# Attention and two expert layers on one core: the weighted sums in fp32, two heads in one pass of the array

## The chip, the cores and the metric

The kernel runs on one core of a Trainium2 chip. The metric is device time in microseconds (us), the median of several runs. The core has five engines with a queue each: TensorE (PE in the profile, with PEld for the loading of its stationary operand), VectorE (DVE), ScalarE (ACT), GpSimd (POOL) and SyncE (SP), which here only starts DMA transfers. SBUF is the working memory of 128 partitions; PSUM is the small memory into which PE writes. An engine works off its queue in order and waits on semaphores for the others.

## The reference

```python
def _attn_ref(q, k, v):                     # (4, 8, 576, 64) each
    q_rot, k_rot = (rotate(q), rotate(k))   # rotary embedding over the 64 columns
    scores = scale * np.matmul(q_rot, k_rot.transpose(0, 1, 3, 2))
    scores = scores - np.max(scores, axis=-1, keepdims=True)
    attn = np.exp(scores)
    attn = attn / (np.sum(attn, axis=-1, keepdims=True) + 1e-09)
    return np.matmul(attn, v).astype(np.float32)

def reference(...):
    x = attention output as (2304, 512)
    h = np.maximum(x @ w_in, 0.0); x = h * h @ w_out           # 512 -> 2048 -> 512
    e_idx = np.argmax(x @ w_gate + modality_bias[modality_id], axis=1)   # 8 experts
    out[mask] = gate_w[mask, None] * (np.maximum(x[mask] @ w1[e], 0.0) @ w2[e])
```

All is fp32, and the choice of the expert depends on small differences, so the kernel keeps close to fp32 throughout: it mostly splits an operand into a high part in the type fp32r and a low part (the rest), and adds up several products.

## The kernel before, in words

**Attention.** The 32 heads are worked in 16 pairs; the two heads of a pair lie in partitions 0 to 63 and 64 to 127. For each pair the program does, by the names in its table:

- `ldq`, `ldk`, `ldv` load; `aq` to `cq` and `ak` to `ck` are the rotary embedding (L213, L215, mostly on POOL); `qh`, `ql`, `kh`, `kl` split into high and low parts, and small transfers `qd`, `kd` move halves to other partitions.
- `sc0` to `sc8` are nine score tiles of 128 rows by 576 columns (L275). Tiles 0 to 3 are head 0, 4 to 7 head 1, tile 8 the 64 last rows of both. They go through two PSUM buffers in turn, in the order 3, 1, 2, 0, 4, 5, 6, 7, 8.
- `mx` takes the maximum of a tile (L280, DVE), `ex` its exponential and the sum of a row (L291, ACT), which frees the PSUM buffer.
- `tr` transposes the exponentials in groups of four 128x128 blocks (L333; L324 for the corner); `m00` to `m13` are eight main groups (first digit the head), `rk`, `rq` and `rr` the remainders. They go through four PSUM buffers called `b`, shared with the weighted sums.
- `eh` copies a group out of PSUM on ACT as the high part, `el` subtracts it on DVE for the low part (L197, L202); both lie in `et0`, `et1` and `rk`. `vhi` (ACT) and `vlo` (POOL) split the values.
- `pv00`, `pv01`, `pv10`, `pv11` are the weighted sums (L367), for head and half of the 576 columns: five chunks of 128 rows times the high and the low part of the exponentials, ten matmuls of 128x288. The stationary operand holds the high part of the values in 64 columns and the low part in 64 more, so the result has two halves that have yet to be added.
- `p1` copies the result out of PSUM (ACT). In pairs 0 to 3 (the first batch row, whose first 512 tokens are block 0 of the next layer) `p2` adds the halves on DVE, and `xn`, `xh`, `xl` normalize and split. In the other pairs `xr` stores both halves, and they are added (`xsum`) when the next layer reads them.
- `sa` (L299, POOL) and `srec` (DVE) prepare the reciprocals of the sums, `sev` and `rst` store them.

What sets the order is a table of times (`FIRST`, `SECOND`, `THIRD`, `PLAN` for pairs 0, 1, 2 and 3, and the rest): a step of pair p stands at its time plus 18 p, all steps are sorted by that number, and each goes into its engine's queue in that order ("T" PE, "V" DVE, "A" ACT, "P" POOL, "D" SP). The numbers are no promise: an engine starts a step when its operands and buffers are ready and the step before it is done.

**Expert layers.** `TAIL` mixes the first layer's weights (loaded as 64-bit floats, put together from two words) into the attention's last pairs. Then the first layer runs over five blocks of tokens, 16 steps each (L706, L740), and the second over the chosen experts (L1024, L1047).

Of the kernel before, what the change touches and what calls it, by code (L numbers as in the profile page):

```python
# [1289 lines left out]
```

## Time and profile before

| | us |
|---|---|
| median of 3 runs | 969.63 (967.72 to 970.1) |
| the profiled execution | 971.64 |
| its span, first to last instruction | 969.9 |
| PE busy | 903.1 (93%) |
| DVE busy | 679.6 (70%) |
| ACT busy | 530.4 (55%) |
| POOL busy | 370.9 (38%) |
| first and last maximum of a score tile | 23.1 and 310.4 |

The attention's steady part lasts from about 140 to 310 us, and the expert layers take the rest. PE's records overlap: matmuls are pipelined, a record lasts longer than the distance to the next, and a busy PE is not necessarily a full one. A wait shown in brackets is idle time of that engine right before the instruction, with the engine and operation that ended it.

### The profile page before, as it was taken

The page shows a single profiled execution, that of the slowest core. Times are in us where ns is not written, and L with a number is a line of the kernel's source. Part 1 is how long each engine was busy: PE and PEld are TensorE (multiplying, and loading weights), DVE is VectorE, ACT ScalarE, POOL GpSimd, SP SyncE. Part 2 cuts the span into 40 slices and gives each one's busy share as a digit, 9 for nine tenths or more (in the row PEclk, how much of TensorE's full clock was granted, in tenths as well). Part 3 has the DMA queues.
Part 4 walks back from the last instruction along what each step waited for, and adds up shares of the span by engine and source line. Part 5 has one row for each costly group of instructions (what it writes and reads, how often), then busy time and mean ns, then how long its engine had stood idle before and what let it go on. Part 6 is the DMA issues. An engine that isn't in the chain of part 4 may idle for free. (4 is left out here: it accounts for less than half of the span.)

```text
span 969.9 us, 15018 instructions
## 1 busy us (share of the span) xinstructions
PE 903.1 (93%) x5210; PEld 789.7 (81%) x5210; DVE 679.6 (70%) x1258; ACT 530.4 (55%) x1090; POOL 370.9 (38%) x287
## 2 busy tenths in 40 slices
PE   0888889999999989999999999999999999999996
PEld 0777888898888866787888888888988889999995
DVE  5789988998989899957647764664473956666650
ACT  3788878888989877532233223222343345555551
POOL 6787877787874466612003100100010124112011
PEclk9999999999999999999999999999999999999998
DMA  7556656746655556562005002100151267777630
GB/s 234 163 147 180 182 146 154 210 139 191 219 150 161 186 181 205 135 197 64 1 1 163 12 1 70 39 1 1 44 177 63 87 194 255 239 229 230 205 107 34
DMA packets 55714, 130.83 MB, mean 135 GB/s; under 512 B 11968, under 2 KB 16592, under 8 KB 55632
## 3 DMA queue, kind: packets, MB, share of 16 engines
q1 hardware_dynamic: 52592, 120.10, 41.3%
q0 software_dynamic: 3040, 9.70, 2.7%
q8 instruction: 43, 0.70, 0.3%
q14 instruction: 39, 0.32, 0.1%
HBM read 97.12 MB, written 19.21 MB: 120 GB/s over the span
## 5 line engine op out<-in xcount | busy, mean ns | idle before, releaser
L712 ACT ACTIVATE r<-h 128x512 f32<-128x512 f32 (+1 forms) x80 | 44.2, 552 | 216.6 <-PE h L706 199.8
L706 PE MATMUL h<-xs,w 128*128 128x512 f32 (+1 forms) x660 | 145.5, 369 | 6.8 <-DVE w L557 5.5
L706 PEld LDWEIGHTS h<-xs,w 128*128 128x128 f32 x660 | 115.1, 188 | 31.9 <-DVE w L557 9.3
L275 PE MATMUL sc<-kh,q 128*128 128x288 f32 (+2 forms) x336 | 98.8, 329 | 36.7 <-ACT kh L197 20.9
L720 DVE SCALAR_TENSOR_TENSOR h<-h,r 128x512 f32<-128x512 f32 (+1 forms) x80 | 51.5, 644 | 113.5 <-ACT r L712 113.2
L740 PE MATMUL y<-w,gh 128*128 128x512 f32 x396 | 122.6, 391 | 0.0
L291 ACT ACTIVATE e<-sc,nmx 128x576 f32<-128x576 f32 x144 | 107.0, 744 | 26.3 <-DVE nmx L280 25.9
L280 DVE TENSOR_REDUCE nmx<-sc 128x1 f32<-128x576 f32 x144 | 106.8, 751 | 17.5 <-PE sc L275 16.5
L978 DVE TENSOR_TENSOR w<-eraw,w 128x1024 fp32r<-128x1024 f32 x64 | 78.4, 1225 | 33.5 <-ACT w L977 33.4
L333 PE MATMUL b<-ident,e 128*128 128x128 f32 x640 | 91.8, 283 | 10.2 <-DVE et L202 4.2
L275 PEld LDWEIGHTS sc<-kh,q 128*128 128x128 f32 x336 | 62.9, 197 | 46.5 <-issue 23.3
L202 DVE TENSOR_TENSOR et<-b,et 128x512 fp32r<-128x512 f32 (+1 forms) x160 | 94.2, 626 | 8.2 <-ACT et L197 6.3
L275 PE MATMUL sc<-kl,q 128*128 128x288 f32 (+2 forms) x336 | 90.7, 304 | 0.0
L333 PEld LDWEIGHTS b<-ident,e 128*128 128x128 f32 x640 | 75.1, 145 | 18.8 <-PE b L324 5.7
L740 PEld LDWEIGHTS y<-w,gh 128*128 128x128 f32 x396 | 73.3, 188 | 14.4
L197 ACT ACTIVATE et<-b 128x512 fp32r<-128x512 f32 (+1 forms) x160 | 83.0, 561 | 2.9 <-PE b L333 2.5
L367 PE MATMUL b<-et,vs 128*128 128x288 f32 x512 | 78.4, 295 | 0.1
L740 PE MATMUL y<-w,gl 128*128 128x512 f32 x198 | 77.1, 389 | 0.0
L1024 PEld LDWEIGHTS h<-ye,w 128*128 128x128 f32 x576 | 74.0, 189 | 3.7
L1054 POOL DMA_INDIRECT out<-ob,six x19 | 21.6, 1138 | 139.8 <-ACT ob L1053 106.8
L752 DVE SCALAR_TENSOR_TENSOR junk<-ysb,wgb 128x512 f32<-128x512 f32 x96 | 75.0, 835 | 0.0
L1024 PE MATMUL h<-ye,w 128*128 128x256 f32 x576 | 74.8, 280 | 0.0
(219 smaller groups left out, 1851.6 us busy)
## 6 DMA issues: line engine op xcount, KB each, us to landing
eraw<-wexp SPq DMA_DIRECT2D x64, 512.0 KB
wraw<-wio SPq DMA_DIRECT2D x32, 512.0 KB
rawq<-qx SPq DMA_DIRECT2D x15, 576.0 KB
rawk<-kx SPq DMA_DIRECT2D x15, 576.0 KB
xT<-xo SPq DMA_DIRECT2D x24, 288.0 KB
kh<-kh SPq DMA_DIRECT2D x45, 144.0 KB
vraw<-v SPq DMA_DIRECT2D x16, 320.0 KB
q<-ql SPq DMA_DIRECT2D x32, 144.0 KB
```

The source lines that it names most:

```text
L197: nc.scalar.activation(out=out, in_=in_, func=ACTF.Copy)
L202: on[eng].tensor_tensor(out=out, in0=in0, in1=f32(hi), op=ALU.subtract)
L275: nc.tensor.matmul(out=o[:, x:x + w], lhsT=q[:, hd, q0:q0 + 128], rhs=k[:, hd, y:y + w], start=(n == 0), stop=(n == len(ops) - 1))
L280: nc.vector.tensor_reduce(out=m, in_=sc(p, j)[:, :, 0:HS], axis=AX.XY, op=ALU.max, negate=True)
L291: nc.scalar.activation(out=e(p)[:, o:o + S].rearrange("p (a b) -> p a b", a=2), in_=sc(p, j)[:, :, 0:HS], func=ACTF.Exp, bias=live[p, f"nm ...
L333: nc.tensor.transpose(t[:, i * 128:(i + 1) * 128], x[:, o:o + 128], ident)
L367: nc.tensor.matmul(out=o, lhsT=lhsT.rearrange("p a b -> p (a b)"), rhs=rhs, start=(c == 0 and i == 0), stop=(c == 4 and i == 1))
L706: nc.tensor.matmul(out=h, lhsT=w[:, a, k * 128:(k + 1) * 128], rhs=xs[b, k][:, c], start=(k == 0 and i == 0), stop=(k == 3 and i == 2))
L740: nc.tensor.matmul(out=yp[t], lhsT=g[a][:, t * 128:(t + 1) * 128], rhs=w[:, c, 512:1024], start=(f == 0 and i == 0), stop=(f == NFC - 1 an ...
L752: nc.vector.scalar_tensor_tensor(out=junk, in0=ysb[j], scalar=1.0, in1=wgb[e], op0=ALU.mult, op1=ALU.mult, accum_out=lg[:, j, e:e + 1])
L978: nc.vector.tensor_tensor(out=w[:, 1], in0=r, in1=f32(w[:, 0]), op=ALU.subtract)
L1024: nc.tensor.matmul(out=h, lhsT=w[:, a, k * 128:(k + 1) * 128], rhs=x[:, c], start=(k == 0 and i == 0), stop=(k == 3 and i == 2))
```

## The change

- The exponentials are copied out of PSUM once, in fp32 (`ev` in place of `eh` and `el`): of the eleven groups, `m02`, `m03`, `m10`, `m11`, `rq` and `rr` by ACT, `m00`, `m01`, `m12`, `m13` and `rk` by DVE (in pairs 4 and on). `et0`, `et1`, `rk`, the values and the result are double buffered.
- The values aren't split (`vhi` and `vlo` go).
- The weighted sums are two groups, `pv0` and `pv1`, one for each half of the columns. A group has ten fp32 matmuls with a stationary operand of 64 columns; head 0 writes partitions 0 to 63, head 1 partitions 64 to 127 of one PSUM tile, and the two heads alternate. The groups stand in the table where `pv10` and `pv11` stood.
- The result is whole: `u0` (DVE) and `u1` (ACT) copy it out, `p2`, the zero fills and `xsum` go, and the store and the later loads move half as much.

Of the table a few entries show what moves:

```diff
-    "trm02": (-69.906, "T"), "mx7": (-69.636, "V"), "ehm02": (-69.532, "A"), "elm02": (-69.257, "V"),
+    "evm02": (-69.532, "A"), "trm00": (-69.043, "T"), "trm03": (-68.699, "T"), "trm01": (-68.235, "T"),
...
-    "pv00": (-61.627, "T"), "elm10": (-61.115, "V"), "elm13": (-60.595, "V"), "pv01": (-60.561, "T"),
-    "rst": (-59.097, "D"), "p101": (-57.141, "A"), "pv10": (-56.563, "T"), "p100": (-56.461, "A"),
+    "rst": (-59.097, "D"), "pv0": (-56.563, "T"), "u0": (-55.931, "V"), "pv1": (-53.486, "T"), "u1": (-52.986, "A"),
```

The code:

```diff
-        rk_t = sb.tile([128, 2, SK], F32R, name="rk", bufs=1)
+        rk_t = [sb.tile([128, SK], F32, name=f"rk{i}", bufs=1) for i in range(2)]
...
-        def vraw(p):
-            return get(p, "vraw", [128, 10, D], F32, 1)
-
-        def vs(p):
-            return get(p, "vs", [128, 10, 2, D], F32R, NVS)
+        def vt(p):
+            return get(p, "v", [128, 10, D], F32, 2)
-            nc.sync.dma_start(out=vraw(p), in_=v[p])
-
-        def vhi(p, eng):
-            copy(eng, vs(p)[:, :, 0], vraw(p))
-
-        def vlo(p, eng):
-            sub(eng, vs(p)[:, :, 1], vraw(p), vs(p)[:, :, 0])
+            nc.sync.dma_start(out=vt(p), in_=v[p])
...
                 nc.tensor.transpose(t[:, i * 128:(i + 1) * 128], x[:, o:o + 128], ident)
 
         def et(p, hd):
-            return get(p, f"et{hd}", [128, 2, 4, S], F32R, 1)
-
-        def evac(p, g):
-            t = tb(p, g)
+            return get(p, f"et{hd}", [128, 4, S], F32, 2)
+
+        def evac(p, eng, g):
+            t, rk = tb(p, g), rk_t[p % 2]
             if g == "rk":
-                return [(t, rk_t[:, :, 64:S])]
-            if g == "rr":
-                return [(t[0:64, 0:64], rk_t[0:64, :, S:640]), (t[0:64, 64:128], rk_t[64:128, :, 0:64])]
-            if g == "rq":
+                parts = [(rk[:, 64:S], t)]
+            elif g == "rr":
+                parts = [(rk[0:64, S:640], t[0:64, 0:64]), (rk[64:128, 0:64], t[0:64, 64:128])]
+            elif g == "rq":
                 t = t.rearrange("p (c x) -> p c x", c=4)
-                return [(t[:, :, 0:64], et(p, 0)[:, :, :, 512:S]), (t[:, :, 64:128], et(p, 1)[:, :, :, 0:64])]
-            hd, c = int(g[1]), int(g[2])
-            return [(t, et(p, hd)[:, :, c, 64 * hd:64 * hd + 512])]
-
-        def ehi(p, eng, g):
-            for t, d in evac(p, g):
-                copy("A", d[:, 0], t)
-
-        def elo(p, eng, g):
-            for t, d in evac(p, g):
-                sub("V", d[:, 1], t, d[:, 0])
-
-        def pv(p, eng, hd, n):
-            o = get(p, f"u{hd}{n}", [128, HS], F32, 4, ps, "b")
-            r0 = 64 * (1 - hd) + n * HS
+                parts = [(et(p, 0)[:, :, 512:S], t[:, :, 0:64]), (et(p, 1)[:, :, 0:64], t[:, :, 64:128])]
+            else:
+                hd, c = int(g[1]), int(g[2])
+                parts = [(et(p, hd)[:, c, 64 * hd:64 * hd + 512], t)]
+            for o, i in parts:
+                copy(eng, o, i)
+
+        def pv(p, eng, n):
+            o = get(p, f"u{n}", [128, HS], F32, 4, ps, "b")
             for c in range(5):
-                for i in range(2):
+                for hd in range(2):
+                    r0 = 64 * (1 - hd) + n * HS
                     if c < 4:
-                        lhsT, rhs = vs(p)[:, 2 * c + hd], et(p, hd)[:, i, c, n * HS:n * HS + HS]
+                        lhsT, rhs = vt(p)[:, 2 * c + hd], et(p, hd)[:, c, n * HS:n * HS + HS]
                     else:
-                        lhsT, rhs = vs(p)[:, 8 + hd], rk_t[:, i, r0:r0 + HS]
-                    nc.tensor.matmul(out=o, lhsT=lhsT.rearrange("p a b -> p (a b)"), rhs=rhs,
-                                     start=(c == 0 and i == 0), stop=(c == 4 and i == 1))
+                        lhsT, rhs = vt(p)[:, 8 + hd], rk_t[p % 2][:, r0:r0 + HS]
+                    nc.tensor.matmul(out=o[64 * hd:64 * hd + 64], lhsT=lhsT, rhs=rhs, start=(c == 0), stop=(c == 4))
 
         def xo(p):
-            return get(p, "xo", [128, 2, S], F32, NXO)
-
-        def pv1(p, eng, hd, n):
-            u, c = live[p, f"u{hd}{n}"], slice(n * HS, n * HS + HS)
-            if p >= 4:
-                copy(eng, xo(p)[:, hd, c], u)
-            else:
-                a, b = 64 * (1 - hd), 64 * hd
-                copy(eng, xo(p)[b:b + 64, 1, c], u[a:a + 64])
-
-        def pv2(p, eng, hd, n):
-            b, c = slice(64 * hd, 64 * hd + 64), slice(n * HS, n * HS + HS)
-            x = xo(p)
-            nc.vector.tensor_tensor(out=x[b, 0, c], in0=live[p, f"u{hd}{n}"][b], in1=x[b, 1, c], op=ALU.add)
-            if n == 1:
-                nc.vector.memset(x[b, 1, N0:S], 0.0)
+            return get(p, "xo", [128, S], F32, 2)
+
+        def take(p, eng, n):
+            copy(eng, xo(p)[:, n * HS:n * HS + HS], live[p, f"u{n}"])
 
         def xr(p, eng):
             b, h = divmod(p, 4)
             if b == 0:
-                nc.sync.dma_start(out=xT[h, :, :, N0:S], in_=xo(p)[:, :, N0:S])
-                return
-            for i in range(2):
-                nc.sync.dma_start(out=xT[h, :, i, b * S:b * S + S].rearrange("(g d) t -> d g t", g=2),
-                                  in_=xo(p)[64 * i:64 * i + 64])
+                nc.sync.dma_start(out=xT[h, :, 0, N0:S], in_=xo(p)[:, N0:S])
+            else:
+                nc.sync.dma_start(out=xT[h, :, 0, b * S:b * S + S], in_=xo(p))
...
         def xraw(b, k):
             t0, n = BLOCKS[b]
             if b == 1:
-                t = wts.pool.tile([128, 2, n], F32, name="xraw", tag="wraw", bufs=NRAW)
-                nc.sync.dma_start(out=t, in_=xT[k, :, :, t0:t0 + n])
-                raws[b, k] = t[:, 0], t[:, 1]
+                t = wts.pool.tile([128, n], F32, name="xraw", tag="wraw", bufs=NRAW)
+                nc.sync.dma_start(out=t, in_=xT[k, :, 0, t0:t0 + n])
+                raws[b, k] = t
                 return
             x = t2([128, n], F32, "xraw")
             if k == 0:
-                rbs[b] = sb.tile([128, 2, n], F32, name="rbs", tag="xs", bufs=5)
-            r, y = rbs[b][:, 0], rbs[b][:, 1]
+                rbs[b] = sb.tile([128, n], F32, name="rbs", tag="xs", bufs=5)
             nc.sync.dma_start(out=x, in_=xT[k, :, 0, t0:t0 + n])
-            nc.sync.dma_start(out=y, in_=xT[k, :, 1, t0:t0 + n])
-            raws[b, k] = x, y
-            xrec(b, k, r)
+            raws[b, k] = x
+            xrec(b, k, rbs[b])
...
-        def xsum(b, k, eng):
-            x, y = raws[b, k]
-            eng.tensor_tensor(out=x, in0=x, in1=y, op=ALU.add)
```

On PE, this is pair 12 before, from the transposes of its last main group (the four of `ident`) on: score tile 0 of the next pair, the first group of weighted sums, tile 4, and the second group (the tile of exponentials `et_3219` is head 0's).

```order
L333 MATMUL b<-ident,e_89 128x128 x4
L275 MATMUL sc<-kh_86,q_84 128x288
L275 MATMUL sc<-kl_88,q_84 128x288
L275 MATMUL sc<-kh_86,q_84 128x288
L275 MATMUL sc<-kl_88,q_84 128x288
L367 MATMUL b<-et_3219,vs 128x288 x8
L367 MATMUL b<-rk,vs 128x288 x2
L275 MATMUL sc<-kh_86,q_84 128x288
L275 MATMUL sc<-kl_88,q_84 128x288
L275 MATMUL sc<-kh_86,q_84 128x288
L275 MATMUL sc<-kl_88,q_84 128x288
L367 MATMUL b<-et_3219,vs 128x288 x8
```

And the same place after, from the last matmul of tile 0 on: tile 4, tile 5, and the first rows of the group `pv0`, whose `et_2708` is head 0's and `et_2777` head 1's.

```order
L245 MATMUL sc<-kl_88,q_84 128x288
L245 MATMUL sc<-kh_86,q_84 128x288
L245 MATMUL sc<-kl_88,q_84 128x288
L245 MATMUL sc<-kh_86,q_84 128x288
L245 MATMUL sc<-kl_88,q_84 128x288
L245 MATMUL sc<-kh_86,q_84 128x288
L245 MATMUL sc<-kl_88,q_84 128x288
L245 MATMUL sc<-kh_86,q_84 128x288
L245 MATMUL sc<-kl_88,q_84 128x288
L332 MATMUL b<-et_2708,v 64x288
L332 MATMUL b<-et_2777,v 64x288
L332 MATMUL b<-et_2708,v 64x288
```

The first group stood between tile 0 and tile 4; now tiles 0, 4 and 5 follow each other, and the group stands behind tile 5, with both heads in turn.

On DVE, the same pair before: the maxima of tiles 5, 6 and 7 (the three in one row), then the subtractions of three groups, the maximum of tile 8, two more, and the maximum of tile 3 of the next pair.

```order
L280 TENSOR_REDUCE nmx<-sc 128x1 x3
L202 TENSOR_TENSOR et_3219<-b,et_3219 128x512 x3
L280 TENSOR_REDUCE nmx<-sc 128x1
L202 TENSOR_TENSOR et_3219<-b,et_3219 128x512
L202 TENSOR_TENSOR rk<-b,rk 128x512
L280 TENSOR_REDUCE nmx<-sc 128x1
L302 RECIPROCAL e_89<-e_89 128x9
L202 TENSOR_TENSOR et_3295<-b,et_3295 128x512
L280 TENSOR_REDUCE nmx<-sc 128x1
L202 TENSOR_TENSOR et_3295<-b,et_3295 128x512
L202 TENSOR_TENSOR et_3219<-b,et_3219 128x4x64
```

And after: the maxima of tiles 5 and 6, the copy of the result of the pair before (`xo`), tile 7, and the copies between the maxima.

```order
L250 TENSOR_REDUCE nmx<-sc 128x1 x2
L178 COPY xo<-b 128x288
L250 TENSOR_REDUCE nmx<-sc 128x1
L178 COPY et_2708<-b 128x512
L250 TENSOR_REDUCE nmx<-sc 128x1
L178 COPY et_2708<-b 128x512
L178 COPY rk_91<-b 128x512
L250 TENSOR_REDUCE nmx<-sc 128x1
L272 RECIPROCAL e_89<-e_89 128x9
L250 TENSOR_REDUCE nmx<-sc 128x1
L178 COPY et_2777<-b 128x512
```

Between the maximum of tile 8 and that of tile 3 there are still two operations (`m01`'s and `rk`'s evacuation), copies now; ahead of tile 8's maximum one remains of three.

## Rows read from the trace of the kernel before

**Rows 1.** windows: busy us of PE, PEld, DVE, ACT, POOL; clock; DMA; GB/s

```profile
139.70:310.40 170.70, 161.53 (x1221) 152.37 (x1222) 154.61 (x256) 153.29 (x383) 127.88 (x97) 1.00 0.60 170
...
440.00:970.00 530.00, 518.03 (x2762) 447.08 (x2762) 304.88 (x641) 195.10 (x328) 69.56 (x60) 0.99 0.31 100
```

**Rows 2.** timeline of POOL: start us, us, engine, line, operation, [idle before]

```profile
139.69 0.24 POOL L299 TENSOR_SCALAR e<-e 128x9 f32<-128x9 f32 x1 [1.93 <-ACT e L291]
...
260.91 0.24 POOL L299 TENSOR_SCALAR e<-e 128x9 f32<-128x9 f32 x1 [0.50 <-ACT e L291]
...
266.88 1.44 POOL L215 TENSOR_TENSOR rawq<-rawq 128x576 f32<-128x576 f32 x1
...
274.13 1.56 POOL L202 TENSOR_TENSOR vs<-vraw,vs 128x640 fp32r<-128x640 f32 x1 [2.03 <-PE b L333]
...
278.07 0.24 POOL L299 TENSOR_SCALAR e<-e 128x9 f32<-128x9 f32 x1 [1.00 <-ACT e L291]
...
312.10 0.24 POOL L299 TENSOR_SCALAR e<-e 128x9 f32<-128x9 f32 x1 [2.65 <-ACT e L291]
```

**Rows 3.** timeline of DVE, the cycle from 261 to 278 us

```profile
268.36 1.66 DVE L199 CAST q<-rawq 128x576 fp32r<-128x576 f32 x1 [0.18 <-POOL rawq L215]
...
276.32 0.75 DVE L280 TENSOR_REDUCE nmx<-sc 128x1 f32<-128x576 f32 x1
```

**Rows 4.** timeline of ACT, the same cycle

```profile
261.82 0.74 ACT L291 ACTIVATE e<-sc,nmx 128x576 f32<-128x576 f32 x1
...
265.27 0.74 ACT L291 ACTIVATE e<-sc,nmx 128x576 f32<-128x576 f32 x1
...
271.52 0.74 ACT L291 ACTIVATE e<-sc,nmx 128x576 f32<-128x576 f32 x1 [0.94 <-DVE nmx L280]
```

**Rows 5.** timeline of PE, the same cycle

```profile
255.25 0.40 PE L275 MATMUL sc<-kh,q 128*128 128x288 f32 x1 [0.44 <-ACT e L291]
...
264.87 1.22 PE L367 MATMUL b<-et,vs 128*128 128x288 f32 x8
...
266.18 0.36 PE L275 MATMUL sc<-kh,q 128*128 128x288 f32 x1
...
268.12 0.29 PE L275 MATMUL sc<-kh,q 128*128 128x288 f32 x1
...
268.65 1.22 PE L367 MATMUL b<-et,vs 128*128 128x288 f32 x8
...
269.97 0.29 PE L275 MATMUL sc<-kh,q 128*128 128x288 f32 x1
...
271.56 0.42 PE L367 MATMUL b<-rk,vs 128*128 128x288 f32 x2
272.40 0.40 PE L275 MATMUL sc<-kh,q 128*128 128x288 f32 x1 [0.42 <-ACT e L291]
...
273.03 1.91 PE L333 MATMUL b<-ident,e 128*128 128x128 f32 x16
274.70 0.51 PE L275 MATMUL sc<-kh,q 128*128 128x288 f32 x2
```

**Rows 6.** groups by line, whole span: busy us, mean ns, then idle before

```profile
L202 DVE TENSOR_TENSOR et<-b,et 128x512 fp32r<-128x512 f32 (+1 forms) x160 | 94.2, 626 | 8.2 <-ACT et L197 6.3 <-PE b L367 1.0
...
L197 ACT ACTIVATE et<-b 128x512 fp32r<-128x512 f32 (+1 forms) x160 | 83.0, 561 | 2.9 <-PE b L333 2.5
```

**Rows 7.** timeline of PE in the early cycles, tile 7 of two pairs

```profile
74.60 0.40 PE L275 MATMUL sc<-kh,q 128*128 128x288 f32 x1 [0.72 <-ACT e L291]
...
132.38 0.40 PE L275 MATMUL sc<-kh,q 128*128 128x288 f32 x1 [2.17 <-ACT e L291]
```

**Rows 8.** line L333, the transposes: what PE waited for, us, times

```profile
  DVE xo L384: 3.5, 7
```

**Rows 9.** by stretch, columns as in Rows 1

```profile
55.00:60.00 5.00, 2.95 (x17) 2.17 (x16) 4.14 (x8) 3.72 (x9) 3.67 (x5) 0.82 1.00 269
...
130.00:135.00 5.00, 2.83 (x17) 2.62 (x16) 3.39 (x5) 3.33 (x8) 2.87 (x3) 0.83 0.78 182
```

More of the change, by code (lines that the diff above doesn't have):

```diff
@@ L27 @@
 N0 = 512
-BLOCK0 = ("p200", "p201", "p210", "p211", "rld", "xn", "xh", "xl", "xst")
+BLOCK0 = ("rld", "xn", "xh", "xl", "xst")
 HS = S // 2
 SK = S + 64
-RAW, NVS, NXO = 1, 1, 1
+RAW = 1
 NT = NTOK // 128
@@ L390, in xr @@
             if b == 0:
-                nc.sync.dma_start(out=xT[h, :, :, N0:S], in_=xo(p)[:, :, N0:S])
-                return
-            for i in range(2):
-                nc.sync.dma_start(out=xT[h, :, i, b * S:b * S + S].rearrange("(g d) t -> d g t", g=2),
-                                  in_=xo(p)[64 * i:64 * i + 64])
+                nc.sync.dma_start(out=xT[h, :, 0, N0:S], in_=xo(p)[:, N0:S])
+            else:
+                nc.sync.dma_start(out=xT[h, :, 0, b * S:b * S + S], in_=xo(p))
         def xn(p, eng):
-            x = xo(p)[:, 0, 0:N0]
+            x = xo(p)[:, 0:N0]
             on[eng].tensor_tensor(out=x, in0=x, in1=rb(p), op=ALU.mult)
@@ L404, in xhi @@
         def xhi(p, eng):
-            copy(eng, xh(p)[:, 0], xo(p)[:, 0, 0:N0])
+            copy(eng, xh(p)[:, 0], xo(p)[:, 0:N0])
         def xlo(p, eng):
-            sub(eng, xh(p)[:, 1], xo(p)[:, 0, 0:N0], xh(p)[:, 0])
+            sub(eng, xh(p)[:, 1], xo(p)[:, 0:N0], xh(p)[:, 0])
         def xst(p, eng):
             nc.sync.dma_start(out=xT[p, :, :, 0:N0], in_=f32(xh(p)))
-        fs = dict(ldv=ldv, vhi=vhi, vlo=vlo, sa=guard, srec=srec, sev=sev, rst=rst, rld=rld, xr=xr, xn=xn, xh=xhi, xl=xlo, xst=xst)
+        fs = dict(ldv=ldv, sa=guard, srec=srec, sev=sev, rst=rst, rld=rld, xr=xr, xn=xn, xh=xhi, xl=xlo, xst=xst)
         for x in "qk":
@@ L426, in attention @@
                 fs[f"{pre}{j}"] = lambda p, eng, f=f, j=j: f(p, eng, j)
-        for pre, f in (("tr", trans), ("eh", ehi), ("el", elo)):
+        for pre, f in (("tr", trans), ("ev", evac)):
             for g in ["rk", "rq", "rr"] + [f"m{h}{c}" for h in range(2) for c in range(4)]:
                 fs[pre + g] = lambda p, eng, f=f, g=g: f(p, eng, g)
-        for pre, f in (("pv", pv), ("p1", pv1), ("p2", pv2)):
-            for h in range(2):
-                for n in range(2):
-                    fs[f"{pre}{h}{n}"] = lambda p, eng, f=f, h=h, n=n: f(p, eng, h, n)
+        for pre, f in (("pv", pv), ("u", take)):
+            for n in range(2):
+                fs[f"{pre}{n}"] = lambda p, eng, f=f, n=n: f(p, eng, n)
         for x in "kq":
@@ L442, in attention @@
             nc.gpsimd.memset(f32(q_buf[i]), 0.0)
-        nc.gpsimd.memset(f32(rk_t), 0.0)
+        for i in range(2):
+            nc.gpsimd.memset(rk_t[i], 0.0)
         for i in range(2):
@@ L619, in xrec @@
             rbs[b, k] = r
-        def xsum(b, k, eng):
-            x, y = raws[b, k]
-            eng.tensor_tensor(out=x, in0=x, in1=y, op=ALU.add)
         def xnorm(b, k, eng):
-            x = raws[b, k][0]
+            x = raws[b, k]
             eng.tensor_tensor(out=x, in0=x, in1=rbs.pop((b, k)), op=ALU.mult)
         def xsplit(b, k):
-            x = raws.pop((b, k))[0]
+            x = raws.pop((b, k))
             n, o = BLOCKS[b][1], OFF * (BLOCKS[b][1] <= SLOT)
@@ L1076, in experts @@
                         e = nc.gpsimd if k < 2 else nc.vector
-                        at(mid, q - 4, lambda b=b, k=k, e=e: xsum(b, k, e), lambda b=b, k=k, e=e: xnorm(b, k, e))
+                        at(mid, q - 4, lambda b=b, k=k, e=e: xnorm(b, k, e))
                     else:
                         at(mid, q - 11 + 2 * k, lambda b=b, k=k: xraw(b, k))
-                        at(mid, q - 10 + 2 * k, lambda b=b, k=k: xsum(b, k, nc.gpsimd),
-                           lambda b=b, k=k: xnorm(b, k, nc.gpsimd))
+                        at(mid, q - 10 + 2 * k, lambda b=b, k=k: xnorm(b, k, nc.gpsimd))
                     at(mid, q - 3, lambda b=b, k=k: xsplit(b, k))
```

192 rows, old and new, of tables (FIRST, PLAN, SECOND, TAIL) are left out of this document.

## The prediction

> **What bounds the kernel now.** I read the busy time by stage first, then one attention cycle in the timeline, engine by engine. From 440 us on TensorE (PE) is busy 518 of 530 us [rows 1]: the two expert layers run on PE, and no other engine matters there. In the attention, 139.7 to 310.4 us, PE, VectorE (DVE) and ScalarE (ACT) are each busy nine tenths of the time and none is full [rows 1]. Such a stage is bound by a ring of waits through several engines, and the reader should look for it. The work of one pair of heads repeats: `sa`, the small operation on the sums (POOL, L299), starts at 260.91 and again at 278.07, a cycle of 17.16 us; from the one at 139.69 to the one at 278.07 there are eight cycles, 17.3 us each [rows 2].
>
> The ring, step by step. After `sa` POOL does five rotary operations; the last starts at 266.88 and takes 1.44 us [rows 2]. The DVE cast of q follows at 268.36, with its wait on POOL shown [rows 3], then the low half of q, then the maximum of score tile 5. ACT stands idle for 0.94 us until that maximum and takes its exponential at 271.52 [rows 4]. PE waits for that exponential and starts score tile 7 at 272.40; its last weighted-sum matmuls began at 271.56, two of them, so it stood idle for 0.6 us [rows 5]. Then come 16 transposes, tile 8 at 274.70 [rows 5], its maximum at 276.32 [rows 3], its exponential, and `sa` at 278.07, with 1.00 us of idle time ended by that exponential [rows 2]. The ring is closed.
>
> **What the change takes away is not in that ring.** Per pair DVE loses 13 subtractions (mean 626 ns) and gets 6 copies; ACT goes from 13 copies of the transposes to 8 (mean 561 ns), loses the copy of the values and three of four copies of the result [rows 6]; POOL loses the low half of the values, 1.56 us at 274.13 [rows 2]. That POOL operation stands between the ring's rotary work and `sa`, and POOL still waits 1.00 us for the exponential after it. The DVE subtractions ahead of tile 8's maximum end just as tile 8 does. So the lighter engines can't make the steady cycle shorter than about 17.1 us: I book nothing for them, and what hides them is the ring.
>
> **What it moves: the weighted sums on PE.** Before, there are four groups of ten matmuls. One group takes 1.32 us, from its first start (268.65) to the next tile's (269.97), so 133 ns a matmul; a score tile of four takes 0.53 us, 268.12 to 268.65 [rows 5]. The first group starts at 264.87, ahead of score tile 4 at 266.18 [rows 5]. It needs head 0 alone, and fills time in which PE would wait: tile 4 needs the buffer of an exponential that ends at 266.01 (265.27 + 0.74) [rows 4]. After the change there are two groups, each with both heads, and they come behind tiles 4 and 5 and behind tile 6. So the first group's 1.33 us lose their cover.
>
> *The cost of one new group.* No row shows a plain fp32 matmul, nor one with 64 stationary columns. Before, exponentials and values each stand as a high and a low part, since one pass doesn't keep fp32; ten passes with 128 stationary columns (64 high, 64 low) make all four products for one head and one half. The same four products without that packing are twice the passes at half the width. If the two heads run abreast, that is 20 passes' time, 20 x 0.133 = 2.66 us a group, and per pair the 5.3 us of now. If one after the other, 5.32 us a group. From below: 16 fp32 transposes of 128 columns go in 1.67 us (273.03 to 274.70), 104 ns each [rows 5]; an fp32 matmul as cheap as one pass makes a group of 20 last 2.66 us in a row, or 1.33 abreast. I take 2.66, at which two of the readings meet; the ends are 1.33 and 5.32.
>
> *The new cycle.* From tile 7 (255.25) to tile 4 (266.18) it is 10.93 us [rows 5]. That stretch runs from tile 8's maximum over two evacuations on DVE and the maximum of tile 3 into an ACT list from 261.82 to 266.01 [rows 4]. Each of these operations keeps its place on its engine (two subtractions become two copies; ACT's list, two exponentials with the small evacuations between, and a third, stays whole). So 10.93 stays. Then come three tiles, 3 x 0.53 = 1.59 us; 0.2 us in which tile 5 waits for its buffer (an exponential of 0.74 against a tile of 0.53); and two groups, 5.32 us: 18.04 us in all. That is more than the ring's 17.16, so PE closes the cycle now: +0.88 us. From `sa` at 139.69 to `sa` at 312.10 there are ten cycles [rows 2]: +8.8 us.
>
> *A switch of the array.* Each group is entered and left with another shape, four times a pair. A matmul's record lasts 0.29 us while the next starts after 0.13 [rows 5], so emptying the array may cost 0.16 us a switch, 4 x 0.16 x 10 = 6.4 us. The rows' other changes of shape, from score tile to transposes and back, show no such step, so I take 0 and keep 6.4 for the range. The Trainium skill, "TensorEngine Tiling (Array Packing)", section Key Properties, says that a change of the tiling mode drains the engine; by that rule the sum would be 982 in place of 976. No row shows it.
>
> *The evacuating copies.* A DVE copy out of PSUM of 128x512 is not in the trace. ACT's takes 561 ns and DVE's subtraction 626 [rows 6]; the cast of q, a DVE copy of 128x576 inside SBUF, takes 1.66 us [rows 3]. I take 0.62, since source and shape are the subtraction's. At the cast's rate (1.66 x 512/576 = 1.48) the two copies ahead of tile 3's maximum would cost 2 x 0.86 us a cycle, 17 us in all; at ACT's rate they gain 1 us in all.
>
> *The early cycles*, until 139.69. PE stands idle before tile 7 for 0.7 to 2.2 us [rows 7], since POOL normalizes block 0 as well; the 1.5 us more on PE's path (0.9 and the 0.6 of idle time used up above) is mostly absorbed. Gains: the additions and zero fills of the second half go, for which PE's transposes waited 3.5 us in seven places [rows 8]; and in two places, four windows of 5 us, the granted clock is 0.82 to 0.83, a mix of 2.4 and 1.2 GHz, after PE was idle for some 2 us [rows 9]. These windows miss 20 x 0.175 = 3.5 us of clock, and a PE with more to do may keep it. I take -3 us, with -7 and +1 as ends.
>
> *The rest.* The last pair's sums stand alone ahead of the expert layer, four old groups against two new ones, 5.3 us each way; the first now waits for head 1 too, +0.3. The 16 additions of the two halves after the attention (14 on POOL, 2 on DVE) and half of the reads that feed them lie beside a full PE [rows 1]: nothing. SP issues one store a pair in place of two; nobody waits for it.
>
> **Sum.** 8.8 - 3 + 0.3 = +6 us on the profiled execution (971.64 us; its span is 969.9): 977.7. The median of the runs shown is 2.0 us under that execution, so 976.
>
> **The rivals.**
> *Serial heads*: the two 64-column matmuls don't overlap, and the change doesn't do what it says. A group takes 5.32 us, the cycle 10.93 + 1.79 + 10.64 = 23.4, so +6.2 x 10 = 62; about +5 in each of five early cycles (6.2 + 0.6 less the idle 0.7 to 2.2), 25; the last pair +5. That is 92 us: 1062 in the median. For it: no row shows two matmuls abreast. Against it: the two heads use different columns of the array and different partitions of PSUM, and follow each other matmul by matmul. Partial overlap lies between. The Trainium skill, "TensorE: Matmul & The Clock Gate", Part 3 (Packing small matmuls), gives 2.38 times for three column tiles side by side, 0.79 of the ideal; by that a group would be 3.4 us as an estimate, the cycle 1.4 us longer, and the time 990. No row shows that either.
>
> *Faster*: a matmul of fp32 operands costs one pass, two abreast, 1.33 us a group. The PE path of the cycle is then 10.93 + 1.79 + 2.66 = 15.4 us, the ring rules at 17.16 again, and what is left are the early cycles (-7) and the last pair (-2.7): 971.6 - 9.7 - 2 = 960. It decides under 2.2 us a group (10.93 + 1.79 + 2 x 2.2 = 17.1). For it: the transposes' 104 ns. Against it: the kernel splits its operands, which would be needless.
>
> *No change*: the lighter DVE and ACT shorten the 10.93 us by the 0.9 us that the groups cost, through waits booked here as unmoved: 971.6 - 3 + 0.3 - 2 = 967. For it: ACT has five copies of the transposes less, some of them ahead of tile 8's exponential. Against it: the list from 261.82 on is back to back and stays.
>
> **How the numbers follow.** Abreast, as forecast: 0.62, own range 968 to 990. Serial: 0.18. Faster: 0.11. No change: 0.09. A measurement of this kernel can tell 0.3% (2.9 us) from no change, so under 966.7 is faster and over 972.5 slower. Of the forecast's 0.62, 0.04 lies below and 0.08 between; of no change 0.01 below. So faster 0.16, same 0.16, slower 0.50 + 0.18 = 0.68. The range starts at 962 (no loss in the cycle, early cycles near their better end) and ends at 1004: 976 + 17 for slow copies + 6.4 for switches + 4 for the early cycles' worse end, which takes in partial overlap too. It leaves out the serial case and a little below.
>
> **What would show it.** Right: `sa` about 18 us apart from 140 us on; no idle PE before tile 7, and instead 1 us or more before tile 4; a group of 2.7 us; DVE and ACT busy six to seven tenths with the cycle no shorter. Wrong: groups of 5 us and cycles of 23 (serial); groups under 2.2 us with cycles of 17.1; or tile 4 sooner than 10.5 us after tile 7, which would mean that the lighter engines had been in the path after all.

## The result and the profile after

The changed kernel takes 975.87 us (median of 11 runs, 973.55 to 980.56) against 971.01 us for the kernel before on the same chip (11 runs, 967.72 to 972.45). The ratio is 1.0061, with a 95% interval of 1.0043 to 1.0078: slower by 0.6%. The profiled execution has a span of 973.6 us, 3.7 more than before.

With the columns of [rows 1], the steady attention:

```profile
135.90:317.00 181.10, 167.65 (x1218) 127.79 (x1218) 124.78 (x187) 117.34 (x293) 110.42 (x87) 0.99 0.54 149
```

DVE is busy 69% of the attention stage and ACT 65%, against nine tenths before, and the stage is no shorter. The timeline of POOL shows the cycle at `sa` (L269 now), as [rows 2] did:

```profile
135.79 0.24 POOL L269 TENSOR_SCALAR e<-e 128x9 f32<-128x9 f32 x1 [1.13 <-ACT e L261]
...
264.29 0.24 POOL L269 TENSOR_SCALAR e<-e 128x9 f32<-128x9 f32 x1 [1.67 <-ACT e L261]
...
282.42 0.24 POOL L269 TENSOR_SCALAR e<-e 128x9 f32<-128x9 f32 x1 [2.17 <-ACT e L261]
...
318.68 0.24 POOL L269 TENSOR_SCALAR e<-e 128x9 f32<-128x9 f32 x1 [6.49 <-ACT e L261]
```

A steady cycle is 18.13 us (264.29 to 282.42) in place of 17.16. The ten cycles from 135.79 to 318.68 take 182.9 us, before 172.4 (139.69 to 312.10). The same cycle on PE, from tile 7 to the next tile 7 (of a tile, the first of its four matmuls, and of tile 6 all four; the rows at 269.50 and 270.22 are tiles 4 and 5):

```profile
258.69 0.40 PE L245 MATMUL sc<-kh,q 128*128 128x288 f32 x1
...
269.50 0.40 PE L245 MATMUL sc<-kh,q 128*128 128x288 f32 x1 [1.31 <-ACT e L261]
...
270.22 0.40 PE L245 MATMUL sc<-kh,q 128*128 128x288 f32 x1
...
270.95 2.16 PE L332 MATMUL b<-et,v 128*64 128x288 f32 x16
272.94 0.66 PE L332 MATMUL b<-rk,v 128*64 128x288 f32 x4
273.52 0.40 PE L245 MATMUL sc<-kh,q 128*128 128x288 f32 x1
273.76 0.29 PE L245 MATMUL sc<-kl,q 128*128 128x288 f32 x1
...
274.02 0.29 PE L245 MATMUL sc<-kl,q 128*128 128x288 f32 x1
274.24 2.16 PE L332 MATMUL b<-et,v 128*64 128x288 f32 x16
276.23 0.66 PE L332 MATMUL b<-rk,v 128*64 128x288 f32 x4
276.81 0.40 PE L245 MATMUL sc<-kh,q 128*128 128x288 f32 x1
```

Read it as a sum: 10.81 us from tile 7 to tile 4, with PE idle for 1.31 us at the end of it; 1.45 for tiles 4 and 5; 2.57 for the first group (270.95 to 273.52); 0.72 for tile 6; 2.57 for the second group. That is 18.12, and nothing waits before tile 7 any more. A group has 20 passes: each of its ten fp32 matmuls stands in the profile as two.

Tile 5 starts 0.72 us behind tile 4, where a tile takes 0.53 [rows 5]: it waits some 0.2 us for its buffer. PE's own row hides that, since a matmul's record outlasts the step to the next; the load of the tile's stationary operand (PEld) shows it. It starts together with the matmul, right behind an exponential of ACT that ends at 270.08:

```profile
269.34 0.74 ACT L261 ACTIVATE e<-sc,nmx 128x576 f32<-128x576 f32 x1
270.22 0.19 PEld L245 LDWEIGHTS sc<-kh,q 128*128 128x128 f32 x1 [0.16 <-ACT e L261]
```

One cycle of the ten is 1.6 us longer. In the windows of PE there (columns as in [rows 1]) the clock goes to half, 1.2 GHz, after PE stood idle, and is back at 2.4 GHz at 181.5 us:

```profile
176.50:177.00 0.50, 0.00 (x0) 0.00 (x0) 0.50 (x2) 0.50 (x2) 0.42 (x2) 1.00 0.00 0
178.50:179.00 0.50, 0.50 (x3) 0.36 (x2) 0.41 (x1) 0.30 (x2) 0.50 (x1) 0.50 0.00 0
181.00:181.50 0.50, 0.50 (x4) 0.24 (x2) 0.47 (x2) 0.00 (x0) 0.00 (x0) 0.50 0.10 23
181.50:182.00 0.50, 0.50 (x6) 0.28 (x4) 0.50 (x2) 0.00 (x0) 0.16 (x1) 0.99 0.96 203
```

After the attention something comes back: the expert layers take 647.2 us (326.43 to the end) in place of 649.9 (from 320.01). PE's waits in their first 120 us, before and then after (us in total, times, longest):

```profile
PE h L706 <- DVE w L557: 5.5, 9, 1.0
PE h L706 <- DVE gl L724: 1.3, 1, 1.3
PE h L706 <- DVE xs L635: 1.2, 1, 1.2
```

```profile
PE h L650 <- DVE w L507: 4.6, 9, 0.5
PE h L650 <- DMA xs<-xT: 0.3, 1, 0.3
PE h L650 <- DVE gl L668: 0.2, 1, 0.2
```

8.0 us of waits have become 5.1. The waits on `gl` and `xs` are the ones that shrink most, and `xs` (L635) is the split of block 1's operands, which stood behind the addition of the two halves. The nine waits on `w` are not the additions' doing: in the kernel before, the last of them ends at 393.32 us, and the first addition (L623) starts at 401.34.

```profile
393.32 3.06 PE L706 MATMUL h<-xs,w 128*128 128x512 f32 x12 [0.54 <-DVE w L557]
401.34 1.74 POOL L623 TENSOR_TENSOR xraw<-xraw 128x512 f32<-128x512 f32 x1
411.38 2.80 PE L706 MATMUL h<-xs,wf 128*128 128x512 f32 x11 [1.18 <-DVE xs L635]
```

### The profile page after: what moved, and what is told of

It is laid out like the page before. It is cut to its first block, busy times and chain, and to the rows that moved or that the text cites. A ratio compares the mean times of both kernels' runs of the same rounds, so it can differ in the third digit from the quotient of the medians.

```text
span 973.6 us, 14639 instructions
## 1 busy us (share of the span) xinstructions
PE 908.2 (93%) x5210; PEld 748.4 (77%) x5210; DVE 615.4 (63%) x1120; ACT 468.8 (48%) x946; POOL 323.1 (33%) x258
## 5 line engine op out<-in xcount | busy, mean ns | idle before, releaser
L245 PE MATMUL sc<-kh,q 128*128 128x288 f32 (+2 forms) x336 | 102.8, 340 | 46.1 <-ACT e L261 25.2
L303 PE MATMUL b<-ident,e 128*128 128x128 f32 x640 | 86.0, 274 | 2.4 <-ACT e L261 2.0
L571 POOL TENSOR_TENSOR xraw<-xraw,rbs 128x512 f32<-128x512 f32 (+1 forms) x14 | 16.6, 1191 | 197.0 <-DMA rbs<-rD 193.5
L991 PE MATMUL y<-w,ge 128*128 128x512 f32 x288 | 74.6, 394 | 0.0
L332 PE MATMUL b<-et,v 128*64 128x288 f32 x512 | 73.0, 425 | 0.1
L921 ACT ACTIVATE w<-eraw 128x1024 fp32r<-128x1024 f32 x64 | 67.3, 1052 | 4.1 <-DMA eraw<-wexp 4.1
```

Of the source, the lines that this page charges most:

```text
L245: nc.tensor.matmul(out=o[:, x:x + w], lhsT=q[:, hd, q0:q0 + 128], rhs=k[:, hd, y:y + w], start=(n == 0), stop=(n == len(ops) - 1))
L303: nc.tensor.transpose(t[:, i * 128:(i + 1) * 128], x[:, o:o + 128], ident)
L332: nc.tensor.matmul(out=o[64 * hd:64 * hd + 64], lhsT=lhsT, rhs=rhs, start=(c == 0), stop=(c == 4))
L921: nc.scalar.activation(out=w[:, 0], in_=r, func=ACTF.Copy)
L991: nc.tensor.matmul(out=yp[s, t], lhsT=g[a][:, t * 128:(t + 1) * 128], rhs=w[:, c, 512:1024], start=(f == 0 and i == 0), stop=(f == EFC - 1 ...
```

## The experiments

My theory: before, a ring over `sa`, POOL, DVE, ACT and PE sets the cycle; after, PE sets it, since the first group of sums lost the wait that it used to fill. The main rivals: the heads don't run abreast; or DVE's and ACT's work, not the ring, set the cycle.

**Do the two heads run abreast?** (`heads_in_turn`)

```diff
-            for c in range(5):
-                for hd in range(2):
+            for hd in range(2):
+                for c in range(5):
```

> The changed kernel, but within a group of weighted sums all ten passes of head 0 stand before the ten of head 1, in place of head by head in turn. The work is the same. In the changed kernel's trace two passes, one of each head, start 7 ns apart and the next two 243 ns later. Theory (the heads run abreast and a pass of 288 columns takes 0.243 us): with the order broken up the 20 passes follow each other at 0.243 us, a group takes 5.0 us in place of 2.57, the cycle 18.13 + 4.9 = 23.0 us, and the time is 1035 to 1062. Rival (a pass takes 0.12 us and the pairs in the trace are only issued together): group 2.6 us, cycle 18.1, time 973 to 980.

Measured: 1021.83 us (2 runs), ratio 1.0533 (1.0504 to 1.0562), cycle 21.16 us. PE's timeline of one group:

```profile
306.62 2.21 PE L332 MATMUL b<-et,v 128*64 128x288 f32 x10
308.62 0.41 PE L332 MATMUL b<-rk,v 128*64 128x288 f32 x1
308.67 0.41 PE L332 MATMUL b<-et,v 128*64 128x288 f32 x1
308.86 0.41 PE L332 MATMUL b<-rk,v 128*64 128x288 f32 x1
308.92 1.38 PE L332 MATMUL b<-et,v 128*64 128x288 f32 x5
...
310.71 0.40 PE L245 MATMUL sc<-kh,q 128*128 128x288 f32 x1
```

The five passes of head 1 at 308.92 follow each other at (1.38 - 0.41) / 4 = 0.243 us: one head alone needs as long for a pass as two heads in turn need for a pair. So they do run abreast, and the doubling is whole. The size was missed: a group is 4.09 us (306.62 to 310.71), not 5.0, since head 1's first passes run beside head 0's last four (308.62 and 308.86 are head 0's, 308.67 is head 1's). 2 x (4.09 - 2.57) = 3.0 us a cycle, which is what the cycle grew by.

**Is PE the end of the cycle now, and what stands behind it?** (`three_chunks`)

```diff
-            for c in range(5):
+            for c in (1, 2, 4):
...
-                    nc.tensor.matmul(out=o[64 * hd:64 * hd + 64], lhsT=lhsT, rhs=rhs, start=(c == 0), stop=(c == 4))
+                    nc.tensor.matmul(out=o[64 * hd:64 * hd + 64], lhsT=lhsT, rhs=rhs, start=(c == 1), stop=(c == 4))
```

> The changed kernel with three of the five chunks of the weighted sums (the sums over chunks 0 and 3 are left out). Each group loses four pairs of passes, 4 x 0.243 = 0.97 us, so the path over PE falls from 18.13 to 16.2 us a cycle. Theory (PE closes the cycle after the change, the ring over POOL, DVE, ACT and PE stands right behind it, at 17.0 to 17.2): cycle 17.0 to 17.2, time 962 to 968. Rival 1 (the lighter VectorE and ScalarE have shortened the ring as well): cycle 16.2 to 16.5, time 953 to 959. Rival 2 (the weighted sums aren't on the path): cycle 18.1, time 973 to 979.

Measured: 965.65 us, ratio 0.996 (0.9944 to 0.9976). `sa` in POOL's timeline:

```profile
220.52 0.24 POOL L269 TENSOR_SCALAR e<-e 128x9 f32<-128x9 f32 x1 [1.04 <-ACT e L261]
...
237.85 0.24 POOL L269 TENSOR_SCALAR e<-e 128x9 f32<-128x9 f32 x1 [0.29 <-ACT e L261]
...
254.85 0.24 POOL L269 TENSOR_SCALAR e<-e 128x9 f32<-128x9 f32 x1 [0.65 <-ACT e L261]
...
289.42 0.24 POOL L269 TENSOR_SCALAR e<-e 128x9 f32<-128x9 f32 x1 [4.55 <-ACT e L261]
```

17.33, 17.00, and 17.3 in the mean of the last two: 1.94 us of passes less gave about 0.9. So PE closed the cycle, and the lighter DVE and ACT didn't shorten what stands behind it. That this is the old ring is read from the waits inside the cycle from 237.85: DVE's cast waits for POOL again, and PE for ACT before tile 7.

```profile
245.22 1.66 DVE L178 CAST q<-rawq 128x576 fp32r<-128x576 f32 x1 [0.51 <-POOL rawq L194]
249.26 0.40 PE L245 MATMUL sc<-kh,q 128*128 128x288 f32 x1 [0.74 <-ACT e L261]
```

**Were the subtractions on the path before?** (`before_no_subtractions`)

```diff
-            for t, d in evac(p, g):
+            for t, d in evac(p, g) if p < 4 else []:
                 sub("V", d[:, 1], t, d[:, 0])
...
-                        lhsT, rhs = vs(p)[:, 2 * c + hd], et(p, hd)[:, i, c, n * HS:n * HS + HS]
+                        lhsT, rhs = vs(p)[:, 2 * c + hd], et(p, hd)[:, i if p < 4 else 0, c, n * HS:n * HS + HS]
...
-                        lhsT, rhs = vs(p)[:, 8 + hd], rk_t[:, i, r0:r0 + HS]
+                        lhsT, rhs = vs(p)[:, 8 + hd], rk_t[:, i if p < 4 else 0, r0:r0 + HS]
```

> The kernel before, without the 13 subtractions of a pair on VectorE in pairs 4 to 15 (the low part of the exponentials is left out, and PE multiplies the high part twice, so that its work is the same). Some 8 us of VectorE's work a pair go. Theory (they aren't in the ring that sets the cycle): cycle 17.0 to 17.2, time 967 to 971. Rival (VectorE bounds the attention, or the two subtractions ahead of tile 3's maximum are in the path): cycle 15.9 to 16.6, time 957 to 964.

Measured: 968.30 us, ratio 0.9983 (0.9965 to 1.0001). `sa`:

```profile
208.51 0.24 POOL L299 TENSOR_SCALAR e<-e 128x9 f32<-128x9 f32 x1 [1.01 <-ACT e L291]
225.65 0.24 POOL L299 TENSOR_SCALAR e<-e 128x9 f32<-128x9 f32 x1 [1.01 <-ACT e L291]
242.83 0.24 POOL L299 TENSOR_SCALAR e<-e 128x9 f32<-128x9 f32 x1 [0.81 <-ACT e L291]
```

17.14 and 17.18: DVE is busy 94.7 of 171 us in place of 154.6 of 170.7, and the cycle is as before.

**Is the ring over `sa` the only one?** (`before_sa_on_vector`; in the changed kernels below the same line)

```diff
-            on[eng].tensor_scalar(out=sums(p), in0=sums(p), scalar1=1e-9, scalar2=None, op0=ALU.add)
+            on["V" if p >= 4 else eng].tensor_scalar(out=sums(p), in0=sums(p), scalar1=1e-9, scalar2=None, op0=ALU.add)
```

> The kernel before, with the small operation on the sums (sa) on VectorE in place of POOL in pairs 4 to 15. POOL's rotary operations then no longer stand behind the exponential of tile 8, and the ring is open. Theory: the cycle falls below 17.16 us, to what the path over PE needs (10.93 us from tile 7 to tile 4, then three tiles of 0.53 and three groups of 1.33, 16.5, and 0.1 to 0.3 for sa on VectorE): 16.5 to 16.9, time 963 to 968. Rival (POOL's order isn't what sets the cycle): 17.1 to 17.4, time 969 to 973.

Measured: 968.83 us, ratio 0.9989 (0.9977 to 1.0002), most steady cycles 17.03 to 17.14 us: neither theory. DVE's timeline shows what came next:

```profile
266.01 0.75 DVE L280 TENSOR_REDUCE nmx<-sc 128x1 f32<-128x576 f32 x1
266.68 1.61 DVE L199 CAST q<-rawq 128x576 fp32r<-128x576 f32 x1
```

The cast no longer waits for POOL (it did for 0.18 us in [rows 3]), and yet starts only when DVE's own list, here a row maximum (L280), is through. That list is a second ring, 0.1 us behind the first.

Both rings hold this cast, and most of its 1.66 us is a wait that the rows don't name. In the kernel before, the cast at 268.36 runs beside a POOL operation that ends at 269.70, and ends at 270.02. The same cast took 0.45 us at 26.76 us, where the POOL operation that was running ended 0.13 us after the cast's start:

```profile
26.76 0.45 DVE L199 CAST q<-rawq 128x576 fp32r<-128x576 f32 x1
...
268.27 1.43 POOL L202 TENSOR_TENSOR kl<-rawk,kh 64x576 fp32r<-64x576 f32 x1
```

In that trace all 15 casts of q end 0.32 us behind the POOL operation during which they started, whatever their length. So some 1.2 us of either ring is the cast standing behind POOL's `kl`; no run here moves `kl` away.

**Both rings at once** (`before_no_sub_sa_vector`: the two edits above together)

> The kernel before with both earlier edits: no subtractions of pairs 4 to 15 (the low part of the exponentials is left out, PE's work is the same), and sa on VectorE. Each edit alone took 0.0 to 0.1 us off the cycle. Theory (two rings stand side by side, the one over sa at 17.16 and VectorE's own full list at 17.04, and each hides what the other would give): together the cycle falls to PE's path, 16.4 to 16.7 us, time 958 to 964. Rival (a third ring, over the load of rawk or ACT's list, at the same height): cycle 16.9 to 17.1, time 965 to 969.

Measured: 964.82 us, ratio 0.9941 (0.9922 to 0.996); the cycles vary between 16.0 and 17.9, 16.9 in the mean of the last ten (17.24 before). Together they give more than either, but less than the theory's 16.4 to 16.7 us and 958 to 964: POOL now waits 6.5 us for loads of rawk between 140 and 300 us (0.2 before).

**The loads** (`before_no_sub_sa_vector_raw2`: meant as the last kernel with two buffers for the loads)

> The kernel before without the subtractions of pairs 4 to 15 (the low part of the exponentials is left out) and with sa on VectorE, and now with two buffers in place of one for the loads of q and k. In the run with the first two edits alone POOL waited 6.5 us for the load of rawk and 2.5 us for that of rawq between 140 and 300 us (0.2 and 1.2 in the kernel before), and the cycles went up and down between 16.0 and 17.9, 17.0 in the mean. Theory (the loads are the third ring: POOL's rotary work frees the one buffer late): the waits for the loads fall under 3 us together, the mean cycle to 16.2 to 16.7, the time to 956 to 963. Rival (the loads wait for their place in SP's queue or for the DMA engines, and not for the buffer): mean cycle 16.8 to 17.1, time 963 to 967.

Measured: 965.23 us, ratio 0.9965 (0.995 to 0.9979), the last ten cycles 16.7 us in the mean, and 7.1 us of POOL's waits for rawk and rawq. This says nothing on the buffer: the kernel that ran is `before_no_sub_sa_vector` letter for letter. Its line 31 still reads `RAW, NVS, NXO = 1, 1, 1`, one buffer. What it does show is how far one kernel's figures lie apart from one series of runs to the next: ratios of 0.9941 and 0.9965, cycles of 16.9 and 16.7 us, waits of 9.0 and 7.1 us. So neither the size of what the two edits give nor the loads as a third ring is settled. A kernel with two buffers comes below, `split_sa_vector_raw2`.

**Filling the idle time** (`split_first_group`: chunks 1, 2 and 4 of the first group, whose exponentials of both heads are there by then, ahead of tile 4)

```diff
+    "pv0a": (-61.600, "T"),
...
-        def pv(p, eng, n):
+        def pv(p, eng, n, chunks=None):
             o = get(p, f"u{n}", [128, HS], F32, 4, ps, "b")
-            for c in range(5):
+            order = (1, 2, 4, 0, 3) if n == 0 and p >= 2 else range(5)
+            for c in chunks or (order[3:] if n == 0 and p >= 2 else order):
...
-                    nc.tensor.matmul(out=o[64 * hd:64 * hd + 64], lhsT=lhsT, rhs=rhs, start=(c == 0), stop=(c == 4))
+                    nc.tensor.matmul(out=o[64 * hd:64 * hd + 64], lhsT=lhsT, rhs=rhs, start=(c == order[0]), stop=(c == order[4]))
...
+        fs["pv0a"] = lambda p, eng: pv(p, eng, 0, (1, 2, 4))
```

> The changed kernel, with the first group of weighted sums in two parts from pair 2 on: chunks 1, 2 and 4 (6 pairs of passes, 1.46 us and 0.14 for the switch) ahead of score tile 4, where PE stands idle for 1.47 us, and chunks 0 and 3 (0.97 + 0.14) behind tile 5, where the whole group stood. The result is the same. Theory (PE closes the cycle, and the idle time ahead of tile 4 is free): tile 4 starts some 0.25 us later, the path over PE is 10.82 + 0.25 + 1.45 + 1.11 + 0.72 + 2.57 = 16.9 us in place of 18.13, and the ring over sa rules again at 17.0 to 17.2; with the drops of the clock behind that idle time gone as well, the time is 962 to 967. Rival (tile 4 moves back by all that the chunks take, or the weighted sums aren't what lengthened the cycle): cycle 17.9 to 18.2, time 972 to 979.

Measured: 963.70 us against 970.2, ratio 0.9931 (0.9906 to 0.9956): faster than both kernels. PE's timeline, from the first part to tile 7:

```profile
275.22 1.19 PE L333 MATMUL b<-et,v 128*64 128x288 f32 x8
276.24 0.66 PE L333 MATMUL b<-rk,v 128*64 128x288 f32 x4
276.83 0.40 PE L245 MATMUL sc<-kh,q 128*128 128x288 f32 x1
...
283.37 0.40 PE L245 MATMUL sc<-kh,q 128*128 128x288 f32 x1 [0.58 <-ACT e L261]
```

Tile 4 has no wait, and most steady `sa` are 17.0 to 17.2 us apart (237.13, 254.30, 271.31 in its trace). This is the most direct evidence for the step that decided: the same weighted sums, with their cover back, and the cycle is as long as in the kernel before.

The wait of 0.58 us before tile 7 belongs to one of the longer cycles, 17.67 us. In most, PE has next to none. Its waits from 140 to 300 us, some nine cycles, in the changed kernel and then here:

```profile
PE sc L245 <- ACT e L261: 11.8, 9, 1.3
```

```profile
PE sc L245 <- DMA q<-ql: 1.8, 3, 0.9
PE sc L245 <- ACT e L261: 1.0, 3, 0.6
```

So the ring doesn't rule again, as the theory had it: PE's own list takes 17.0 us in this order (16.9 forecast), beside the ring's 17.16, and the steady cycle is no better than before. Most of the gain on the kernel before is in the early cycles, whose end (the `sa` before the last ten cycles) is at 133.4 us in place of 139.7. Of these 6.3 us, 3.4 are the clock that the kernel before misses in two stretches at half clock, at 58 and 133 us; here the granted clock is full in all of the attention's cycles.

**Split, and `sa` on VectorE** (`split_and_sa_on_vector`)

> The same with sa on VectorE in pairs 4 to 15 as well, which opens the ring over POOL. VectorE has fewer operations than in the kernel before, so its own list should not close at 17.04 us as it does there. Theory: the cycle is what the path over PE needs, 16.9 to 17.0 us (some 0.15 under the kernel with the split alone), time 960 to 966. Rival (a further ring stands at 17.1): the same time as with the split alone, within 1 us.

Measured: 964.52 us, ratio 0.9938 (0.9914 to 0.9963): the same as with the split alone, as the rival said. PE waits 4.3 us in all between 140 and 300 us, so its own list of 17.0 us is what remains, and opening the ring can't help. POOL waits 7.8 us for rawk there. With two buffers for the loads (`split_sa_vector_raw2`: `RAW = 2`, and one buffer for the transposed exponentials):

> The changed kernel with the first group split and sa on VectorE, with two buffers for the loads of q and k, and for room one in place of two for the transposed exponentials. Theory (loads as the third ring, PE's path at 16.9 behind it): mean cycle 16.7 to 17.0 in place of 17.1, time 960 to 964. Rival (the loads wait for SP's queue or the DMA engines, or the single buffer of the exponentials makes a new wait): mean cycle 17.0 to 17.3, time 963 to 968.

Measured: 961.97 us against 968.8, ratio 0.9925 (0.9911 to 0.994), the last ten cycles 17.1 us in the mean. By the ratios it can't be told from the split alone. Here the two buffers are in the kernel, and they don't shorten POOL's waits: 7.0 us for rawk (7.8 with one) and 26.8 for rawq (26.2). SP's own wait for the buffer, 2.2 us with one, is gone. In SP's list the loads stand behind transfers of `kh`, for which SP waits 25.4 us for ACT in both kernels; that this place in the list holds the loads up fits the trace, and was not tested.

**Do the additions of the halves cost nothing?** (`before_no_halves_added`)

```diff
         def xsum(b, k, eng):
             x, y = raws[b, k]
-            eng.tensor_tensor(out=x, in0=x, in1=y, op=ALU.add)
```

> The kernel before without the 16 additions of the two halves of the attention's result in the first expert layer (xsum; the second halves are left out of the sum). The prediction booked their removal at nothing. Theory (they stand ahead of the split of block 1's operands, for which PE waits 1.2 us, and they take up VectorE in block 0, where PE waits 5.5 us for weights): PE waits 5 to 6.5 us in the first 120 us of the expert layers in place of 8.0, and the time falls by 1 to 3 us, to 966.5 to 968.5. Rival (beside a full PE they cost nothing): waits of 8 us, time 969 to 970.

Measured: 968.44 us against 970.2, ratio 0.9979 (0.9964 to 0.9993). PE's waits in the first 120 us of the expert layers:

```profile
PE h L705 <- DVE w L557: 4.6, 9, 0.6
PE h L705 <- DMA xs<-xT: 0.3, 1, 0.3
```

4.9 us, close to the changed kernel's 5.1, in place of 8.0. The additions were on the path, but not for all of these 3.1 us. The 1.2 us on `xs` stand in all five profiled executions with the additions and in none of the seven without: these are theirs. Two of those five have no wait on `gl` at all, and the waits on `w` come before any addition, so the theory's second half (the additions crowd VectorE in block 0) is wrong. By the medians the gain is 1.8 us, with an interval of 0.7 to 3.5.

## Why the prediction was right, and where it was not

The time came out as forecast, and the likeliest case is the one that happened: the heads run abreast, PE closes the cycle, and the kernel is slightly slower. That the number fits so well is partly luck. Between the two profiled executions the ten cycles cost 10.5 us (8.8 forecast), the early cycles give back 3.9 (3 forecast), the last pair gives back 0.2 (0.3 of cost forecast), and the expert layers give back 2.7 (nothing forecast): +3.7 us in place of +6. The medians differ by 4.9. The forecast of 976 started from a median of 969.6; over eleven runs that kernel has 971.0.

- *The ring; the lighter engines gain nothing.* Right: `before_no_subtractions` and `three_chunks`. It was taken for the only ring; DVE's list stood 0.1 us behind it (`before_sa_on_vector`). This changed no term of the sum.
- *The first group loses its cover, and PE closes the cycle.* Right: 18.04 us forecast, 18.13 measured; `three_chunks` and `split_first_group` show it. Of the +10.5 us in ten cycles (forecast +8.8), 1.6 are the one stretch at half clock, which was not in the sum.
- *The 10.93 us from tile 7 to tile 4 stay.* Right: 10.81.
- *A group of 2.66 us.* Right in size, 2.57. The passes are cheaper than taken: a pair, one of each head, goes in 0.243 us against 2 x 0.133, so 20 pairs a cycle save 0.46 us. The serial rival and partial overlap are refuted by `heads_in_turn`, the cheap pass by the same 0.243.
- *The switch of the array, taken as 0.* Wrong. In the PE rows after, entering a group takes 0.22 us from the last score matmul (274.02 to 274.24) where matmuls of one shape follow at 0.13; leaving it takes 0.34 from the last pair (0.243 after the one at 276.23, so 276.47 to 276.81) where pairs follow at 0.243; and the first score matmul then takes 0.24 (273.52 to 273.76) in place of 0.13. That is 0.3 us a visit, two visits a cycle, 6 us in ten cycles; 0.11 a cycle of it, tile 7's first matmul, stood in the 10.93 already. The upper end kept for the range, 6.4, was the right size. The Trainium skill, "TensorEngine Tiling (Array Packing)", Key Properties, said that a change of the mode drains the engine; these rows agree. Of the first matmul's 0.11, the rows show why: before, the load of tile 6's stationary operand starts 0.13 us ahead of the matmul (269.84 and 269.97), here together with it (273.52). A wait does the same: tile 4 behind its wait has 0.24 as well (269.50 to 269.74). A visit changes type and shape at once. The transposes, fp32 too, follow a score tile after 0.13 us (277.32 to 277.45), which speaks for the shape. What made up for the switches are the faster passes (0.46 a cycle) and the shorter way from tile 7 to tile 4 (0.12).
- *Tile 5 waits 0.2 us for its buffer.* Right: 0.19 (269.50 to 270.22, less 0.53).
- *The copies on DVE, 0.62 us.* They take what the subtractions took: 0.68 on average, the subtractions of 128x512 also 0.68. The 626 ns of [rows 6] is a mean over two shapes; the row says so (+1 forms). The cast's 1.66 us was no rate to fear: most of it is the wait behind POOL told above.
- *The early cycles, -3 us.* The size was right (139.69 became 135.79, -3.9), a reason was not: the clock fell twice again, at 82 and 103 us in place of 58 and 133, so that nothing was gained there. The other reason was smaller than booked: of the 3.5 us of [rows 8], PE itself waited 1.3, and the rest is its weight loads, counted beside it. The gain lies before the first `sa` (1.1 us) and in the first and the last early cycle (3.0 and 1.8), and the three between lose 2.1; its cause stays open.
- *The last pair, +0.3.* From `sa` to the expert layers it is 7.75 us, before 7.91: -0.2.
- *The additions of the halves, booked at nothing beside a full PE.* Wrong. The row of 440 us and later was read for all of it; in the first 120 us of the layer PE is not full, and waits for DVE. In the profiled executions 2.7 us came back there, which is part of why the span grew by 3.7 us when the attention ended 6.4 us later. 1.2 us of them are shown to be the additions' (the wait on `xs`); `before_no_halves_added` gives 1.8 by the median.

## What to carry to other kernels

When several engines are nine tenths busy and none is full, look for the ring and ask of each moved instruction which wait it was filling; merging two groups into one that starts when the later operand is there can cost all that the merged work takes. Before booking a removal as hidden beside a full engine, read that engine's waits in the very stretch in which the removed work stands. When a group no longer fits into a wait, cut it along its operands, and put what is ready into the gap. And where an operation's length varies on the same shape, look at what another engine does beside it before taking the length for a rate.

## What the runs showed of the hardware

- Two fp32 matmuls of 64 stationary columns on different halves of the columns run wholly abreast: a pair of passes in 0.243 us, one alone in 0.243. An fp32 pass of 288 columns takes 1.8 times the 0.133 us of an fp32r one, and a matmul needs two.
- PE starts matmuls for the other half of the columns while earlier ones of the first half are still waiting their turn (`heads_in_turn`: 308.67 starts ahead of 308.86, which stands before it in the program). So the sentence that an engine works off its queue in order doesn't hold for PE there; alternating the heads in the program still pays, 2.57 us a group in place of 4.09.
- A DVE cast of 128x576 inside SBUF doesn't finish while a POOL operation runs that started before it: it ends 0.32 us behind it, and takes from 0.45 to 1.69 us accordingly (15 casts of q in the kernel before). DVE's copies out of PSUM show nothing of the kind, 0.62 to 0.69 us.
- A stretch at half clock lengthens a steady cycle by 1.6 us each time in these profiles (19.73 in place of 18.13; 22.76 and 22.75 in place of 21.17). In the attention's steady cycles such stretches occur in the changed kernel (178 us) and in `heads_in_turn` (155 and 219 us), where PE is idle for about 1.3 us ahead of tile 4 in each cycle; not in the nine profiled executions whose cycles lack that wait, and not in `three_chunks`, which has it. So such a gap may bring it on and need not.
